# An ALiBi table built ahead of all attention, used by batch 1 in place of a bias matmul, and attention units that start earlier

## The chip, the cores and the metric

The kernel runs on one core of a Trainium2 chip. The metric is the time of one execution on the device in microseconds (us). The five engines of the core run side by side and wait for each other by semaphores: TensorE (PE, and PEld for its weight loads), VectorE (DVE), ScalarE (ACT), GpSimd (POOL) and SyncE (SP). Each takes its instructions in the order in which the program lists them.

## The reference

The inputs q, k and v are random fp32 of 8 batches, 8 heads, 576 positions and 64 columns; w_in is 512 x 2048 and w_out 2048 x 512.

```python
scores = (q @ k.T) / 8                        # for each batch and head
rel    = pos[:, None] - pos[None, :]
bias   = slopes[:, None, None] * -abs(rel)    # slopes[h] = 2 ** -(h + 1)
scores = where((rel >= 0) & (rel < 128), scores + bias, -1e9)
attn   = softmax(scores) @ v                  # sliding window of 128 keys
x      = attn.transpose(0, 2, 1, 3).reshape(4608, 512)
h      = x @ w_in                             # 4608 x 2048
out    = where(h > 0, h, exp(min(h, 0)) - 1) @ w_out
```

A query sees itself and the 127 keys before it. So a block of 128 keys meets 256 queries, and within these 256 columns the bias depends on the head alone.

## The kernel before

**Attention.** A batch has four units. Unit u holds, for all 8 heads, 128 keys by 256 queries (unit 3: 128 by 192 and the last 64 keys by 64). The scores of a unit go from TensorE into PSUM banks (spa, sp2, sp3), ScalarE writes their exponential to EX[u] in fp16 (L164, L169, L186), and TensorE multiplies by v with a column of ones (`values`, L207, result av). VectorE takes the reciprocal of the sum (L213) and normalises into xn (L214). `turn` transposes xn into the ring xT, by TensorE and a copy (L228, L229) for batch 0 and most of batch 1, by a transposing DMA issued on SP (L222) for the rest.

**Two ways of adding the bias.** Batches 0 and 1 go through `first_scores`. For each half of the heads it puts slope times RB, the masked distances, into the bank with four matmuls of 256 columns against SI, a scaled identity (L153), and adds q k to it (L159). Batches 2 to 7 go through `scores` and `expo` without a bias, and VectorE multiplies EX by a table of exponentials TAB afterwards (`weigh`, L191). TAB is made by ScalarE from RB, one activation for each head (`table`, L324), in slots 18 to 21.

**The MoE part.** 9 tiles of 512 tokens. `hidden` multiplies a step of x by w_in into one of the banks hp (L246; in early slots sp2 as well), ScalarE takes the exponential e (L251), POOL clamps it in place (L252), and VectorE makes g (L259, `elu`), which frees the bank. `output` multiplies four chunks of g by w_out (L268); after four such steps ScalarE copies the bank op to ob (L272) and SP sends it out.

**The order.** It is written out by hand. The program is a list of slots, one for each step of `hidden`: 16 slots to a tile of tokens, slot 16 t + j for step j of tile t. In a slot come first what `before` has put there (exponentials of attention), then `hidden`, then `elu` of the step one or two slots earlier, then what `at` has put there (scores, weighs, values, turns, loads), and at last `output`, whose step runs 17 slots behind `hidden`. The fourth of its four steps falls on every slot whose number is a multiple of 4.

A batch from 2 on has a start slot in START. Its unit u has scores at START[b] + 4 u, exponentials in the two slots behind, a weigh in each of the same two, values in the two after these, and the turn with the second values; a fifth block of values follows unit 3 two slots later. The K and Q transposes on VectorE (`turn_qk`, L131) come 8 to 1 slots before START[b], the loads of q, k and v, issued on POOL, 16 to 3 slots before it. Batch 1's units start at slots 10, 12, 14 and 16.

**The start.** POOL makes index tables with iota and issues the first loads; VectorE makes ident, RB and SI; TensorE runs 80 matmuls on ident (`warm`, L278), then transposes the first q and k (`turn_first`, L123), which VectorE and ScalarE copy to KT and QT (L127).

## Time and profile before

| | |
|---|---|
| median of 7 runs | 337.15 us (335.54 to 337.86) |
| the profiled execution | 336.41 us, span 334.6 us |
| granted TensorE clock in it | 1.0 |
| TensorE (PE) busy | 320.1 us, 96% |
| VectorE (DVE) busy | 214.2 us, 64% |
| ScalarE (ACT) busy | 184.5 us, 55% |
| POOL busy | 166.1 us, 50% |

The profile is one execution. A row of its timeline has the start in us, the duration in us, the engine, the line of the kernel, the operation, output and input with their shapes, how many instructions were merged, and in brackets the idle time of the engine before it with what ended that. The span is the time from the first instruction to the last; the execution's own time is 1.8 us longer.

### The profile page before, as it was taken

The page shows a single profiled execution, that of the slowest core. Times are in us where ns is not written, and L with a number is a line of the kernel's source. Part 1 is how long each engine was busy: PE and PEld are TensorE (multiplying, and loading weights), DVE is VectorE, ACT ScalarE, POOL GpSimd, SP SyncE. Part 2 cuts the span into 40 slices and gives each one's busy share as a digit, 9 for nine tenths or more (in the row PEclk, how much of TensorE's full clock was granted, in tenths as well). Part 3 has the DMA queues.
Part 4 walks back from the last instruction along what each step waited for, and adds up shares of the span by engine and source line. Part 5 has one row for each costly group of instructions (what it writes and reads, how often), then busy time and mean ns, then how long its engine had stood idle before and what let it go on. Part 6 is the DMA issues. An engine that isn't in the chain of part 4 may idle for free.

```text
span 334.6 us, 9249 instructions
## 1 busy us (share of the span) xinstructions
PE 320.1 (96%) x3884; PEld 226.2 (68%) x3884; DVE 214.2 (64%) x433; ACT 184.5 (55%) x325; POOL 166.1 (50%) x257
## 2 busy tenths in 40 slices
PE   8999989999997999899999999999999999999995
PEld 8777757767675667666667666666776666766542
DVE  5547546776697767886689667976699666644300
ACT  1666658756664566546565666656554666444311
POOL 8658756226664465535656465726665222333200
PEclk9999999999999999999999999999999999999999
DMA  8999999116999299946999298937999111110121
GB/s 108 197 197 166 194 191 91 12 41 90 118 113 69 56 132 108 103 73 89 123 90 101 58 124 107 109 83 107 122 98 89 55 50 49 47 41 31 50 78 63
DMA packets 93641, 31.99 MB, mean 96 GB/s; under 512 B 81824, under 2 KB 88992, under 8 KB 93600
## 3 DMA queue, kind: packets, MB, share of 16 engines
q0 software_dynamic: 73344, 18.36, 67.3%
q1 hardware_dynamic: 20256, 13.05, 15.1%
q8 instruction: 30, 0.49, 0.6%
q14 instruction: 11, 0.09, 0.1%
HBM read 36.70 MB, written 9.44 MB: 138 GB/s over the span
## 4 chain that ended last, share of the span: by engine, by line
PE 83%; DVE 5%; DMA 5%; ACT 3%; issue 2%; POOL 1%; DVEq 0%; ACTq 0%; POOLq 0%; SPq 0%
PE hp L246 32%; PE op L268 31%; DMA xT<-xn 5%; PE av L207 5%; PE spa L180 3%; PE spare L278 2%; PE hp L268 2%; PE spa L153 2%; DVE g L259 1%; DVE xn L214 1%; ACT e L251 1%; PE spa L159 1%; POOL e L252 1%; PE tp L123 1%; DVE KT L131 1%
## 5 line engine op out<-in xcount | busy, mean ns | idle before, releaser
L252 POOL TENSOR_SCALAR e<-e 128x512 f32<-128x512 f32 x144 | 89.5, 622 | 143.2 <-ACT e L251 142.5
L246 PEld LDWEIGHTS <-wi 128*128 128x128 f16 x1600 | 121.0, 98 | 43.1 <-issue 4.3
L246 PE MATMUL hp<-xT,wi 128*128 128x256 f16 (+3 forms) x1504 | 145.1, 245 | 3.1 <-DMA xT<-xn 2.9
L268 PE MATMUL op<-wo,g 128*128 128x512 f16 x544 | 138.6, 379 | 1.2 <-ACT ob L272 1.2
L251 ACT ACTIVATE e<-hp 128x512 f32<-128x512 f32 x139 | 83.3, 600 | 95.4 <-PE hp L246 91.9
L259 DVE SCALAR_TENSOR_TENSOR g<-e,hp 128x512 f16<-128x512 f32 x139 | 93.7, 674 | 65.6 <-POOL e L252 65.2
L268 PEld LDWEIGHTS <-g 128*128 128x128 f16 x576 | 50.6, 97 | 44.8 <-issue 5.4
L100 POOL DMA_DIRECT2D VP<-in_v_dram x40 | 35.1, 878 | 1.0 <-issue 0.7
L191 DVE TENSOR_TENSOR EX<-EX,TAB 128x1024 f16<-128x1024 f16 x48 | 32.8, 684 | 4.0 <-ACT EX L186 4.0
L214 DVE TENSOR_TENSOR xn<-av,rden 128x256 f16<-128x256 f32 (+1 forms) x79 | 33.4, 423 | 2.9 <-DVE rden L213 0.3
L207 PE MATMUL av<-VP,EX 128*128 128x65 f16 x572 | 30.0, 193 | 2.3 <-issue 1.1
L272 ACT COPY ob<-op 128x512 f32<-128x512 f32 x34 | 19.9, 585 | 20.9 <-PE op L268 20.9
L207 PEld LDWEIGHTS <-EX 128*128 128x128 f16 x576 | 26.6, 98 | 4.1 <-issue 1.7
L186 ACT ACTIVATE EX<-spa 128x512 f16<-128x512 f32 x48 | 26.1, 595 | 4.0 <-PE spa L180 3.4
L186 ACT ACTIVATE EX<-sp 128x512 f16<-128x512 f32 x48 | 26.1, 600 | 0.0
L213 DVE RECIPROCAL rden<-av 128x4 f32<-128x4 f32 (+1 forms) x79 | 13.9, 176 | 18.8 <-PE av L207 17.9
L131 DVE STREAM_TRANSPOSE KT<-st 128x576 f16<-128x576 f16 x24 | 19.6, 817 | 0.0
L131 DVE STREAM_TRANSPOSE QT<-st 128x576 f16<-128x576 f16 x24 | 19.6, 815 | 0.0
L164 ACT ACTIVATE EX<-spa 128x1024 f16<-128x1024 f32 (+1 forms) x16 | 13.9, 867 | 6.9 <-PE spa L159 6.8
L94 POOL DMA_DIRECT2D st<-in_q_dram x24 | 16.4, 682 | 1.0 <-DMA wo<-in_moe_w_out_dram 0.9
L94 POOL DMA_DIRECT2D st<-in_k_dram x24 | 16.4, 685 | 0.1
L180 PE MATMUL sp<-QT,KT 32*128 32x256 f16 (+2 forms) x240 | 14.7, 248 | 0.0
(62 smaller groups left out, 148.0 us busy)
## 6 DMA issues: line engine op xcount, KB each, us to landing
out_dram<-ob SPq DMA_DIRECT2D x36, 256.0 KB, 2.3
VP<-in_v_dram POOLq DMA_DIRECT2D x32, 128.0 KB, 4.6
st<-in_k_dram POOLq DMA_DIRECT2D x24, 144.0 KB, 3.6
st<-in_q_dram POOLq DMA_DIRECT2D x24, 144.0 KB, 3.7
wi<-in_moe_w_in_dram POOLq DMA_DIRECT2D x4, 512.0 KB, 11.3
wo<-in_moe_w_out_dram POOLq DMA_DIRECT2D x4, 512.0 KB, 10.3
s<-in_k_dram POOLq DMA_DIRECT2D x2, 384.0 KB, 9.7
s<-in_q_dram POOLq DMA_DIRECT2D x2, 384.0 KB, 10.2
```

What stands on the lines that cost most here:

```text
L94: nc.gpsimd.dma_start(st[b][32 * g:32 * g + 32, w, :, :, :, :].rearrange("p h n j d -> p (h n) (j d)"), (q, k)[w][b, 2 * g:2 * g + 2, :, : ...
L100: nc.gpsimd.dma_start(VP[b % 2][0:p, n, :, 0:D], v[b, :, 128 * n:128 * n + p, :].rearrange("h p d -> p h d"))
L131: V.transpose(o, st[b][:, w, h2, n0:n1, :, 32 * dh:32 * dh + 32])
L186: nc.scalar.activation(unit(b, u)[:, g, :, :], sp[g].rearrange("p (h c) -> p h c", h=2), AF.Exp, scale=0.125)
L191: V.tensor_tensor(out=e, in0=e, in1=TAB[:, int(u == 3), 2 * gp:2 * gp + 2, :, :], op=ALU.mult)
L207: nc.tensor.matmul(a[:, x, h2, :], ex_[u][:, c:c + 128], VP[b % 2][:, n, 2 * g + h2, 0:D + 1], start=j == 0, stop=j == len(parts) - 1)
L214: V.tensor_tensor(out=o, in0=a[0:m, :, :, 0:D], in1=r[0:m].unsqueeze(3).broadcast_to([m, 2, 2, D]), op=ALU.mult)
L246: nc.tensor.matmul(p[:, l * w + u0:l * w + u1], w_in_sb[:, c, fc * 128:(fc + 1) * 128], xT[:, c, x0:x0 + u1 - u0], start=(c == 0), stop=(c ...
L251: nc.scalar.activation(e[:, 0:n], p[:, 0:n], AF.Exp)
L252: nc.gpsimd.tensor_scalar(out=e[:, 0:n], in0=e[:, 0:n], scalar1=1.0, scalar2=0.0, op0=ALU.min, op1=ALU.max)
L259: V.scalar_tensor_tensor(out=gs[t][:, f0:f0 + nf, c0:c0 + w], in0=sh(es.pop((t, c0, f0))), scalar=1.0, in1=sh(hps.pop((t, c0, f0))), op0=A ...
L268: nc.tensor.matmul(o, gs[t][:, fc, ts * 128:(ts + 1) * 128], w_out_sb[:, fc, :], start=(fc == 0), stop=(fc == NFC - 1))
```

## The change

Three things change. First, RB is made from 256 columns in fp16 on VectorE, from the 128 columns of `col` that ident already needs; the other columns are copied, and three iota of POOL go. Second, the eight table activations stand ahead of the warm-up matmuls and all attention, and batch 1 and unit 3 of batch 0 take no bias matmuls: a new `first_weigh` multiplies their exponentials by TAB on VectorE, one slot after the scores of each half (both halves in slot 5 for batch 0). Third, START of batch 3 comes one slot sooner and that of batches 4 to 7 two slots sooner.

```diff
         def first_scores(b, u, half, d):
...
-            r0 = 256 * int(u == 3)
-            for x, hh in heads:
+            added = b == 0 and u < 3
+            for x, hh in heads if added else []:
                 c = 256 * (x % 2)
-                nc.tensor.matmul(sp[2 * d + hh][:, c:c + 256], SI[:, 4 * hh + x, :], RB[:, r0:r0 + 256],
+                nc.tensor.matmul(sp[2 * d + hh][:, c:c + 256], SI[:, 4 * hh + x, :], RB[:, 0:256],
                                  start=x % 2 == 0, stop=False, skip_group_check=True)
...
-                                     start=False, stop=True, skip_group_check=True)
+                                     start=not added, stop=True, skip_group_check=True)
...
+        def first_weigh(b, u, half):
+            e = unit(b, u)[:, half::2, :, :]
+            V.tensor_tensor(out=e, in0=e, in1=TAB[:, int(u == 3), half::2, :, :], op=ALU.mult)
...
-        rel = one([128, 512], I32, "rel")
...
-        for c, n in ((0, 256), (256, 192), (448, 64)):
-            nc.gpsimd.iota(rel[:, c:c + n], pattern=[[1, n]], base=0, channel_multiplier=-1)
...
-        ra = one([128, 512], F32, "ra")
-        V.tensor_scalar(out=ra, in0=rel, scalar1=0.0, scalar2=BIG, op0=ALU.is_lt, op1=ALU.mult)
-        V.tensor_tensor(out=ra, in0=ra, in1=rel, op=ALU.add)
-        rb = one([128, 512], F32, "rb")
-        V.tensor_scalar(out=rb, in0=ra, scalar1=127.0, scalar2=BIG, op0=ALU.is_gt, op1=ALU.mult)
-        V.scalar_tensor_tensor(out=RB, in0=ra, scalar=-1.0, in1=rb, op0=ALU.mult, op1=ALU.subtract)
+        rel = one([128, 256], F16, "rel")
+        off = one([128, 256], F16, "off")
+        V.tensor_scalar(out=rel[:, 0:128], in0=col, scalar1=rowf, scalar2=None, op0=ALU.subtract)
+        V.tensor_scalar(out=rel[:, 128:256], in0=rel[:, 0:128], scalar1=128.0, scalar2=None, op0=ALU.add)
+        V.tensor_scalar(out=off, in0=rel, scalar1=0.0, scalar2=-BIG, op0=ALU.is_lt, op1=ALU.mult)
+        V.tensor_tensor(out=off, in0=off, in1=rel, op=ALU.subtract)
+        V.tensor_scalar(out=rel, in0=rel, scalar1=127.0, scalar2=-BIG, op0=ALU.is_gt, op1=ALU.mult)
+        V.tensor_tensor(out=RB[:, 0:256], in0=off, in1=rel, op=ALU.add)
+        V.tensor_copy(RB[:, 256:448], RB[:, 0:192])
+        V.tensor_copy(RB[:, 448:512], RB[:, 0:64])
...
+        for h in range(H):
+            table(h)
         warm(80)
...
+        at(5, first_weigh, 0, 3, 0)
+        at(5, first_weigh, 0, 3, 1)
...
-        for h in range(H):
-            at(18 + h // 2, table, h)
...
                 at(a + half, first_scores, 1, u, half, 0)
                 before(a + half + 1, first_expo, 1, u, half, 0, 0, 256)
+                at(a + half + 1, first_weigh, 1, u, half)
                 at(a + half + 2, values, 1, u, half)
...
-        START = [None, None, 25, 41, 59, 77, 95, 113]
+        START = [None, None, 25, 40, 57, 75, 93, 111]
```

## The prediction

> **What bounds it now.** I read the page first, then the waits, then the chain that ended last, then the timeline around the code that changes.

> ```profile
> PE 320.1 (96%) x3884; PEld 226.2 (68%) x3884; DVE 214.2 (64%) x433; ACT 184.5 (55%) x325; POOL 166.1 (50%) x257
> ...
> PE hp L246 <- DMA xT<-xn: 2.9, 2, 1.9
> ...
> 100.08 6.11 DMA xT<-xn
> ```

> TensorE is the bound: 14.5 us of idle in 334.6, so only its own work, or what makes it wait, counts. The second line is from the waits: two stalls on a transposing transfer, the longest 1.9 us. I number slots by the runs of L246: slot 12 starts at 42.93 us, 19 at 60.75, 40 at 106.23, 56 at 140.48, and a late slot without attention takes 1.74. Slot 15, where batch 1 runs, is in the timeline (start, duration, engine, line):

> ```profile
> 51.39 1.07 PE L246 MATMUL hp<-xT,wi 128*128 128x128 f16 x16
> 51.56 1.02 ACT L164 ACTIVATE EX<-spa 128x1024 f16<-128x1024 f32 x1 [0.22 <-PE spa L159]
> ...
> 52.30 0.40 PE L207 MATMUL av<-VP,EX 128*128 128x65 f16 x8
> 52.50 0.60 ACT L251 ACTIVATE e<-hp 128x512 f32<-128x512 f32 x1
> ...
> 52.64 0.60 PE L153 MATMUL spa<-RB,SI 128*128 128x256 f16 x4
> 52.74 0.18 DVE L213 RECIPROCAL rden<-av 128x4 f32<-128x4 f32 x1 [0.77 <-PE av L207]
> 52.95 0.42 DVE L214 TENSOR_TENSOR xn<-av,rden 128x256 f16<-128x256 f32 x1
> 53.17 0.39 PE L159 MATMUL spa<-QT,KT 64*128 64x256 f16 x4
> ...
> 53.30 0.68 DVE L259 SCALAR_TENSOR_TENSOR g<-e,hp 128x512 f16<-128x512 f32 x1
> ```

> TensorE goes from one row to the next; VectorE has 1.3 us of work in a 2.1 us slot. L153 is what the change takes out.

> **Bias matmuls out, weighs in.** From L153 to L159 is 0.53 us, and 0.10 of it is the change of row groups, which stays: 0.43 us for four matmuls. Ten halves lose them (two of batch 0, eight of batch 1): 4.3 us at most. Each gets a multiply on VectorE of the form that L191 has (128x1024, mean 684 ns), between exponential and values. What waits behind it on VectorE: the next clamp-and-max (L259), reciprocal and normalisation, and behind those TensorE's next values. VectorE's rows overlap: L259 starts at 95.04 and the weigh after it at 95.65. So a slot costs VectorE 0.61 (L259) + 0.21 + 0.35 (L213 to L214 to the next) + 0.60 (weigh) = 1.8 us, against TensorE's 0.9 hidden + 0.25 values + 0.5 scores with its gaps + 0.1 for a turn in every second slot = 1.75. The two are level, so some is lost. By place:
> - Batch 0's last unit, slots 4 to 7: TensorE already waits there for xn (0.11 at 26.92), and two weighs stand ahead of the L259 that frees a bank for slot 7. Followed through the queues: -0.1, not -0.86.
> - Batch 1's first half, slot 10: -0.4. Its second: L159 waits 0.51 at 42.61 for the copy of KT, which hides the bias: 0. Third: -0.43. So -0.9 at slot 13.
> - The other five, slots 13 to 17: 5 x 0.43 = 2.15, less some 0.2 in each second slot where values wait for the weigh: -1.6. That is -2.5 at slot 18.

> **Given back in slot 19.** Two values share one bank there, and the next bank but one is ScalarE's:

> ```profile
> 61.86 0.40 PE L207 MATMUL av<-VP,EX 128*128 128x65 f16 x8
> ...
> 63.00 0.42 PE L207 MATMUL av<-VP,EX 128*128 128x65 f16 x8 [0.74 <-DVE xn L214]
> ...
> 65.70 1.14 ACT L324 ACTIVATE TAB<-RB 128x512 f16<-128x512 f16 x2
> ...
> 67.21 0.60 ACT L272 COPY ob<-op 128x512 f32<-128x512 f32 x1
> ...
> 67.86 1.02 PE L268 MATMUL op<-wo,g 128*128 128x512 f16 x4 [0.46 <-ACT ob L272]
> ```

> The last weigh of batch 1 comes ahead of a transpose of K and this normalisation on a VectorE with no idle since 60.30: the second values start 0.7 later, +0.7. The tables leave slots 18 to 21; with them goes the wait of 0.46 at 67.86 and a restart of about 0.1: -0.6. Front in all: -2.4.

> **The table at the start.** Eight activations, 1.14 a pair: 4.6 us. VectorE's chain to RB is now eight operations after 1.56 us. Their nearest rows are 0.15 (SI, 128 fp16 columns) and 0.85 (512 fp32 columns, L311); half of that for half the columns gives 0.15 to 0.45, so RB at 2.8 to 5.2 and the table at 7.4 to 9.8. I take 0.25 each, since the operands are short and fp16. ScalarE's first copy starts at 9.99, after the 80 warm-up matmuls end at 9.07, so it is hidden at both ends; without that cover it would cost 4.6. The three iota that go (0.74 on POOL) let loads start 0.7 sooner, but no load ends a wait of TensorE there: 0.

> **The moved units.** With a unit go its scores, exponentials, weighs, values, turn, loads and K/Q transposes. Batch 2 stays at slot 25.
> - Slots 48 and 56 wait 0.07 and 1.07 for the turn of a batch 3 unit, which comes one slot (1.74) sooner: -1.1.
> - Slot 40 waits 1.86 for batch 2's turn, not moved. But its 6.11 us lie beside two 128 KB loads of V for batch 3; one slot sooner, the second of them is the 64 KB one. Turns beside V loads took 2.3 to 5.5. The gain is 0 to 1.86, and below nothing if two other loads meet there (+0.3); I take -1.0.
> - Slot 43 now has both batch 2's last values and batch 3's first in one bank, as slot 19 has: 1.14 from start to start, less 0.25 of work: +0.9.
> - Batch 3's scores move from slots 41, 45, 49, 53 to 40, 44, 48, 52. Every fourth slot ends an output group, so ScalarE's copy ob (L272), which waits for that output, now stands ahead of the exponentials. Such a queue is in the trace at batch 4, for the second pair of heads:

> ```profile
> 167.24 0.58 ACT L272 COPY ob<-op 128x512 f32<-128x512 f32 x1 [0.31 <-PE op L268]
> 167.72 1.09 ACT L186 ACTIVATE EX<-sp 128x512 f16<-128x512 f32 x2
> ...
> 168.69 0.62 ACT L251 ACTIVATE e<-hp 128x512 f32<-128x512 f32 x1
> ```

> For the first pair: scores slot's first matmul at P, output ends P+2.8, ob P+2.9, exponentials P+3.4, e P+4.3, POOL's clamp P+5.0, L259 P+5.7 to P+6.4, and only then is the hp bank of the slot three later free, due at P+6.1. Wait 0.3, and 0.4 where a transpose of K or Q stands in VectorE's queue: +1.1 over slots 47, 51, 55 (43 has slack). Bounds: 0 (ScalarE catches up) and 0.75 each.
> - Batches 4 to 7 swap the positions 3, 1, 3, 1 (slot modulo 4) for 1, 3, 1, 3, and TensorE is full there: 0.

> **Sum.** -2.4 - 1.1 - 1.0 + 0.9 + 1.1 = -2.5. The profiled execution took 336.41 (span 334.6, 1.8 around it): it should become 333.9. The median of the runs, 337.15, is 0.74 above it; moved alike it is 334.6.

> [...] The clamp on POOL and a weigh met once in full:

> ```profile
> 112.61 1.26 POOL L252 TENSOR_SCALAR e<-e 128x512 f32<-128x512 f32 x1 [2.02 <-ACT e L251]
> 112.73 0.67 DVE L191 TENSOR_TENSOR EX<-EX,TAB 128x1024 f16<-128x1024 f16 x1
> ```

> The clamp took 1.26 and not 0.62, although it began first; all 48 weighs took 0.67 to 0.69. I charge the meeting to the clamp, which has a slot of slack. [...] Secondly, L259 runs until 95.73 and the weigh behind it starts at 95.65. [...]

> **Rivals.**
> - *VectorE keeps up*: nothing is held in slots 13 to 19, and all of batch 1's bias but the hidden half comes through: -3.0 - 0.1 - 0.6 instead of -2.4, with the rest as above: -3.8, 333.3; with no ob queue either, -4.9, 332.2. For it: VectorE at 60% from 50 to 60 us. Against: its loop is as long as TensorE's. 0.13.
> - *The weigh is held by the clamp* (slower). In slots 11 to 18 the exponential ends just when e is clamped (48.25 and 48.85 in slot 13), so they meet in every slot. 0.65 (1.26 less 0.61) on each of eight weighs, on the loop that values wait for: +5.2, in all +2.7, 339.8. It decides from 0.31 per weigh on (2.5/8). Against: no weigh of 48 was long, and batch 2 to 7 meet too. 0.13.
> - *Batch 3's position costs all that is won* (no change). Slots 47, 51 and 55 at 0.75 instead of 0.35 (+1.2), slot 43 also in the queue (+0.5), and slot 40 keeps its wait (+1.0): +2.7, so +0.2, 337.3. For it: the order on ScalarE is written in the code. 0.16.

> **Numbers.** Forecast 0.58, rivals 0.13, 0.13, 0.16. A measurement of this kernel tells about 0.3% (1.0 us) from no change. Forecast and first rival are nearly all faster; of the third, most is same: faster 0.72, same 0.15, slower 0.13. The range leaves out the first rival's far end and most of the second: 332.6 to 337.3.

> **To check.** L153 has 24 matmuls; slots 14 to 17 take 1.75 to 1.85 instead of 2.1 to 2.3; the two values of slot 19 lie 1.8 apart; no wait for ob at slot 21; no wait for xT at slot 56, but one for av at slot 43 and for hp at 47, 51, 55. Wrong if the rows of the added weigh are longer than 0.7 or the first copy of ScalarE starts after 10.0.

## The result, and the profile after

| | before | after |
|---|---|---|
| median of the runs, us | 336.75 (31 runs, 335.17 to 337.86) | 334.11 (12 runs, 332.36 to 335.15) |
| ratio, 95% interval | | 0.9919 [0.9902, 0.9935] |
| profiled execution, us (span) | 336.41 (334.6) | 332.67 (330.9) |

The change made the kernel faster by 0.8%; 334.6 was forecast. In the profiled execution the gain is 3.74 us where the sum said 2.5, in the medians 2.6. The two differences have causes of their own, found below.

The new function moves most lines behind it 4 further down: L246 is now L250, L207 L211, L214 L218, L259 L263, L272 L276, and L324 is L330; the new weigh is L175. First the page's line of engines, then three rows of the waits (us in total, times, longest).

```profile
PE 316.0 (96%) x3844; PEld 223.4 (68%) x3844; DVE 219.0 (66%) x447; ACT 182.8 (55%) x325; POOL 168.5 (51%) x254
```

```profile
PE av L211 <- DVE xn L218: 2.4, 2, 1.4
...
PE hp L250 <- DMA xT<-xn: 1.1, 2, 0.9
PE spa L159 <- DVE KT L127: 1.1, 1, 1.1
```

TensorE has 40 matmuls less (the ten halves of L153) and is busy 4.1 us less, VectorE 4.8 more. The waits for the transposing transfers fell from 2.9 to 1.1; the wait for a normalised unit rose from 0.7 to 2.4. In the chain that ended last the two turns before slots 32 and 40 stand like this (start, duration; before, the second took 6.11):

```profile
80.16 5.10 DMA xT<-xn
...
97.44 4.42 DMA xT<-xn
```

The end of slot 14 and slot 15 (from 48.26) in the timeline, with VectorE's chain and POOL's clamp:

```profile
46.81 1.15 POOL L256 TENSOR_SCALAR e<-e 128x512 f32<-128x512 f32 x1 [0.36 <-ACT e L255]
46.81 0.68 DVE L175 TENSOR_TENSOR EX<-EX,TAB 128x1024 f16<-128x1024 f16 x1
...
47.41 0.68 DVE L263 SCALAR_TENSOR_TENSOR g<-e,hp 128x512 f16<-128x512 f32 x1
...
48.04 0.18 DVE L217 RECIPROCAL rden<-av 128x4 f32<-128x4 f32 x1
...
48.26 0.42 DVE L218 TENSOR_TENSOR xn<-av,rden 128x256 f16<-128x256 f32 x1
48.26 1.07 PE L250 MATMUL hp<-xT,wi 128*128 128x128 f16 x16
...
48.60 0.81 DVE L175 TENSOR_TENSOR EX<-EX,TAB 128x1024 f16<-128x1024 f16 x1
48.87 1.01 POOL L256 TENSOR_SCALAR e<-e 128x512 f32<-128x512 f32 x1
49.34 0.68 DVE L263 SCALAR_TENSOR_TENSOR g<-e,sp 128x512 f16<-128x512 f32 x1
49.45 0.62 ACT L255 ACTIVATE e<-hp 128x512 f32<-128x512 f32 x1
49.47 0.29 PEld L211 LDWEIGHTS <-EX 128*128 128x128 f16 x8 [0.32 <-DVE EX L175]
```

From L263 to L263 VectorE needs 1.93 us and has no idle; the slot takes 1.88. Where a clamp and a weigh met, the clamp paid and sometimes both did: the clamps took 1.15 and 1.01 instead of 0.61, the weighs 0.68, which is as short as any, and 0.81. The last row is the values' wait for a weigh.

The start, and slot 19:

```profile
1.48 0.28 DVE L311 TENSOR_SCALAR rel<-col,rowf 128x128 f16<-128x128 int32 x1
...
3.54 0.30 DVE L318 COPY RB<-RB 128x64 f16<-128x64 f16 x1
...
3.88 4.26 ACT L330 ACTIVATE TAB<-RB 128x512 f16<-128x512 f16 x8 [1.86 <-DVE RB L318]
...
9.94 0.80 ACT L127 COPY QT<-hp 128x768 f16<-128x768 f16 x1 [1.79 <-PE hp L123]
```

```profile
57.44 0.68 DVE L175 TENSOR_TENSOR EX<-EX,TAB 128x1024 f16<-128x1024 f16 x1
58.04 0.82 DVE L131 STREAM_TRANSPOSE KT<-st 128x576 f16<-128x576 f16 x1
...
58.18 0.42 PE L211 MATMUL av<-VP,EX 128*128 128x65 f16 x8
58.76 0.65 DVE L263 SCALAR_TENSOR_TENSOR g<-e,hp 128x512 f16<-128x512 f32 x1
...
59.53 0.42 DVE L218 TENSOR_TENSOR xn<-av,rden 128x256 f16<-128x256 f32 x1
...
60.02 0.42 PE L211 MATMUL av<-VP,EX 128*128 128x65 f16 x8 [1.42 <-DVE xn L218]
```

The table is done at 8.14, 1.79 us before ScalarE's first copy. In slot 19 the first values wait for the weigh, and their normalisation stands behind a transpose of K and a clamp-and-max: the second values come 1.84 after the first.

### The profile page after: what moved, and what is told of

Its sections match the earlier page's. It is cut to its first block, busy times and chain, and to the rows that moved or that the text cites. A ratio compares the mean times of both kernels' runs of the same rounds, so it can differ in the third digit from the quotient of the medians.

```text
span 330.9 us, 9178 instructions
## 1 busy us (share of the span) xinstructions
PE 316.0 (96%) x3844; PEld 223.4 (68%) x3844; DVE 219.0 (66%) x447; ACT 182.8 (55%) x325; POOL 168.5 (51%) x254
## 3 DMA queue, kind: packets, MB, share of 16 engines
q1 hardware_dynamic: 20256, 13.05, 14.5%
## 4 chain that ended last, share of the span: by engine, by line
PE 75%; DVE 7%; DMA 7%; ACT 4%; issue 3%; POOL 3%; DVEq 0%; ACTq 0%; POOLq 0%
PE op L272 31%; PE hp L250 29%; PE av L211 4%; PE spa L184 3%; DMA wo<-in_moe_w_out_dram 3%; DMA xT<-xn 3%; DVE g L263 2%; POOL e L256 2%; PE spare L282 2%; PE hp L272 2%; DVE xn L218 1%; ACT EX L190 1%; ACT e L255 1%; DMA VP<-in_v_dram 1%; DVE KT L131 1%
## 5 line engine op out<-in xcount | busy, mean ns | idle before, releaser
L256 POOL TENSOR_SCALAR e<-e 128x512 f32<-128x512 f32 x144 | 92.8, 645 | 136.7 <-ACT e L255 135.8
L250 PEld LDWEIGHTS <-wi 128*128 128x128 f16 x1600 | 121.2, 98 | 42.3 <-issue 6.7
L250 PE MATMUL hp<-xT,wi 128*128 128x256 f16 (+3 forms) x1504 | 144.8, 245 | 1.7 <-DMA xT<-xn 1.1
L272 PE MATMUL op<-wo,g 128*128 128x512 f16 x544 | 138.6, 379 | 0.7 <-ACT ob L276 0.7
L263 DVE SCALAR_TENSOR_TENSOR g<-e,hp 128x512 f16<-128x512 f32 x139 | 93.6, 674 | 62.2 <-POOL e L256 60.8
L272 PEld LDWEIGHTS <-g 128*128 128x128 f16 x576 | 50.7, 97 | 44.3 <-issue 4.8
L218 DVE TENSOR_TENSOR xn<-av,rden 128x256 f16<-128x256 f32 (+1 forms) x79 | 33.4, 423 | 2.7
L276 ACT COPY ob<-op 128x512 f32<-128x512 f32 x34 | 19.9, 585 | 23.8 <-PE op L272 23.8
L211 PE MATMUL av<-VP,EX 128*128 128x65 f16 x572 | 29.9, 193 | 3.2 <-DVE xn L218 2.4
L211 PEld LDWEIGHTS <-EX 128*128 128x128 f16 x576 | 26.2, 98 | 5.5 <-DVE xn L218 2.6
L164 ACT ACTIVATE EX<-spa 128x1024 f16<-128x1024 f32 (+1 forms) x16 | 14.0, 876 | 3.1 <-PE spa L159 3.0
```

The costliest lines, as they stand in the source:

```text
L211: nc.tensor.matmul(a[:, x, h2, :], ex_[u][:, c:c + 128], VP[b % 2][:, n, 2 * g + h2, 0:D + 1], start=j == 0, stop=j == len(parts) - 1)
L218: V.tensor_tensor(out=o, in0=a[0:m, :, :, 0:D], in1=r[0:m].unsqueeze(3).broadcast_to([m, 2, 2, D]), op=ALU.mult)
L250: nc.tensor.matmul(p[:, l * w + u0:l * w + u1], w_in_sb[:, c, fc * 128:(fc + 1) * 128], xT[:, c, x0:x0 + u1 - u0], start=(c == 0), stop=(c ...
L256: nc.gpsimd.tensor_scalar(out=e[:, 0:n], in0=e[:, 0:n], scalar1=1.0, scalar2=0.0, op0=ALU.min, op1=ALU.max)
L263: V.scalar_tensor_tensor(out=gs[t][:, f0:f0 + nf, c0:c0 + w], in0=sh(es.pop((t, c0, f0))), scalar=1.0, in1=sh(hps.pop((t, c0, f0))), op0=A ...
L272: nc.tensor.matmul(o, gs[t][:, fc, ts * 128:(ts + 1) * 128], w_out_sb[:, fc, :], start=(fc == 0), stop=(fc == NFC - 1))
```

## Where the time went, slot by slot

Differences of slot lengths between the two profiled executions, beside the terms of the sum. A slot is counted here from its first weight load, so a wait ahead of its first matmul is in it where that load had already begun.

| place | forecast | measured |
|---|---|---|
| batch 0, unit 3 (start of slot 7) | -0.1 | -0.10 |
| slot 10 | -0.4 | -0.44 |
| slot 11 | 0 | -0.08 (the wait for K's copy grew from 0.51 to 1.06) |
| slot 12 | -0.43 | -1.71 (a stall of 1.10 is gone) |
| slots 13 to 17 | -1.6 | -1.62 |
| slot 19 | +0.7 | +1.02 |
| slot 21 | -0.6 | -0.62 |
| front (start of slot 22) | -2.4 | -3.61 |
| wait before slot 32 | 0 | +0.96 |
| wait before slot 40 | -1.0 | -1.69 |
| slot 43 | +0.9 | +0.98 of wait |
| slots 47, 51, 55 | +1.1 | +1.04 (0.31, 0.37, 0.36) |
| waits before 48 and 56 | -1.1 | -1.14 |
| to the end | -2.5 | -3.74 |

The rows leave -0.28 over, which no single place shows: it is spread over work that now sits in other slots and batches 4 to 7. In slots 47, 51 and 55 the 0.24 of values that moved there from other slots is taken out first: slot 47 grew from 1.74 to 2.29, less 0.24 leaves 0.31.

## The experiments

The theory was the sum's: the front gains by the bias matmuls' going, and the move of the units gives and takes about the same. Rivals: the weigh is held by the clamp; the move alone, or a stall that the sum had left out, makes the time. Ratios are against the kernel before, timed beside each run.

**Front and units apart.** First the changed kernel with the positions of before.

```diff
-        START = [None, None, 25, 40, 57, 75, 93, 111]
+        START = [None, None, 25, 41, 59, 77, 95, 113]
```

> The table at the start and the weighs in place of batch 1's bias matmuls, with the start slots of before. The prediction's sum gives the front -2.4 us, and slot 40 and 56 keep the waits of before (1.9 and 1.1): about -2.4 against before. If the stall of 1.1 us in slot 12 of the profile of before is chance and not part of the change, the timed difference stays near -2.4 while a profile may show up to -3.6 at slot 22. Rival (VectorE keeps up): -3.7. Rival (the weigh is held by the clamp): above 0.

Measured: 334.45 us, 0.9952 [0.9931, 0.9974]. Then the kernel before with the new positions (the same line the other way):

> The kernel before with only the new start slots. Prediction's parts: waits of slots 48 and 56 gone (-1.1), slot 40's wait shorter (-1.0, in the profile of the changed kernel -1.7), two values in one bank at slot 43 (+0.9, in that profile +1.3), ob ahead of the exponentials at slots 47, 51, 55 (+1.1, in that profile +1.8): -0.1 by the prediction, +0.2 by the profile of the changed kernel. Rival (batch 3's position costs all that is won): +2.5 or more.

Measured: 336.27 us, 1.0013 [0.9992, 1.0033]. So the front carries the gain, but less of it than the sum's 2.4: alone it brings 1.6, the move alone costs 0.4, which the interval does not tell from nothing, and both together bring 2.7 (0.0081 of 336): more than their sum. The waits say why. TensorE's row for the transposing transfers in the run with the front alone, and one more wait, before slot 88, that the profile names otherwise although it ends 0.09 us after such a transfer has landed (203.20):

```profile
PE hp L250 <- DMA xT<-xn: 3.0, 3, 1.5
```

```profile
203.29 1.03 PE L250 MATMUL hp<-xT,wi 128*128 128x256 f16 x8 [1.05 <-DVE KT L131]
```

With the front alone TensorE waits 4.1 us for transfers, where the kernel before waits 2.9; with the units moved as well it waits 1.1. From slot 22 to the end the front alone so gives back 1.04, and the changed kernel gives back nothing (-0.13).

**Batch 3 one slot later** in the changed kernel (40 becomes 41 in START), and then also its V loads one slot sooner:

> The changed kernel with batch 3 at slot 41 as before; batches 4 to 7 keep their new slots. If the ob queue and the shared bank of values are what slots 43, 47, 51, 55 cost (3.0 us in the profile of the changed kernel), all four waits go; slot 56 gets back about 1.1 and slot 40 up to 1.7, since V loads come a slot later: -0.3 against the changed kernel, and no wait for hp at slots 47 to 55. If the waits came from something else (the DMA or VectorE's load in general), they stay and the time rises by 1 to 2.8 us.

Measured: 333.0 us, 0.9915 [0.9888, 0.9943]. Slots 43, 47 and 51 are back at 1.98, 1.74 and 1.76, as forecast, and the waits for transfers are back as well (first row below): no difference from the changed kernel that the intervals show.

```diff
-                at(a - 12 + n if b == 2 else a - 7 + n, load_v, b, n)
+                at(a - 12 + n if b == 2 else a - 7 - (b == 3) + n, load_v, b, n)
```

> As the run with batch 3 at slot 41, but its five V loads are issued one slot sooner, in the slots that they have in the changed kernel. If slot 40's wait is set by which V load lies beside batch 2's turn, the wait stays at 0 to 0.4 us as in the changed kernel: 1.3 us faster than the run before it, -1.6 against the changed kernel. If the V loads do not set it, the same as the run before it.

Measured: 332.74 us, 0.9917 [0.9886, 0.9949]. A miss: the waits moved to other slots (0.25 before slot 40, 1.20 before 48, 1.87 before 56) and their sum stayed. The rows of the two runs:

```profile
PE hp L250 <- DMA xT<-xn: 3.1, 3, 1.6
```

```profile
PE hp L250 <- DMA xT<-xn: 3.3, 3, 1.9
```

So the term "-1.0 at slot 40, by another V load beside the turn" has the wrong cause. The wait at slot 40 is 0.13 to 0.34 in all seven traces of kernels without batch 1's bias matmuls whose turn there is a transfer, also with the front alone, where units and V loads stand as before (0.34); it is 1.26 to 1.86 in all five traces with them, also where the units have moved (1.34). The fall belongs to the front. What in the front brings it is below, under "Why a transfer is late".

**The start alone, and the weighs alone.** The kernel before with the new RB and the table ahead of attention; then the same with the ten weighs added while the bias matmuls stay, so that the bias counts twice.

```diff
+        at(5, first_weigh, 0, 3, 0)
+        at(5, first_weigh, 0, 3, 1)
...
+                at(a + half + 1, first_weigh, 1, u, half)
```

> The changed kernel's start alone: RB from 256 fp16 columns and the table ahead of attention, while batch 1 and batch 0's unit 3 keep their bias matmuls, no weigh is added and the units stand where they stood before. By the prediction's sum only the table's leaving slots 18 to 21 counts: -0.6 us against the kernel before (slot 21 loses its wait for ob), nothing at the start, slots 13 to 17 stay at 2.1 to 2.3 and slot 19 at 3.15 less what the table held. Rival (start not hidden): ScalarE's first copy later than 10.0 us and every slot later by as much. Of the stall of 1.1 us that TensorE shows in slot 12 of the kernel before with nothing that it waits for: if it belongs to the longer code of the bias matmuls it stays here (slot 12 about 4.1); if it was made by what stood on POOL's queue (three iota) it goes and the time falls by 1.7.

Measured: 336.11 us, 1.0002 [0.998, 1.0024]. The profile has -0.61 at slot 22, all of it slot 21 (2.38 to 1.76), and no delay at the start; in the time it can't be seen. The stall stays (1.22 at 46.18), so neither the table nor POOL's three iota made it.

> The same, and the ten weighs of batch 1 and of batch 0's unit 3 are added although the bias matmuls stay, so the bias counts twice in these units. What the weighs cost by themselves, against the run without them: by the prediction +0.7 in slot 19 and some 0.2 in each second slot of 13 to 17, and some 0.7 at slots 4 to 7 of batch 0: +1.5 to +2.3 us. If the weigh is held by POOL's clamp (second rival): 0.65 on each of eight weighs, +5 us. If VectorE keeps up (first rival): under +0.8, with slot 19 as before.

Measured: 336.31 us, 1.0015 [0.9991, 1.0039]. Slots 13 to 17 are as long as before (2.10, 2.23, 2.10, 2.27, 2.71); slot 19 takes 3.71 instead of 3.15:

```profile
L175 DVE TENSOR_TENSOR EX<-EX,TAB x10: 681/688/1043, 28.0 to 60.3; 128x1024 f16<-128x1024 f16 x10
```

```profile
62.98 0.42 PE L211 MATMUL av<-VP,EX 128*128 128x65 f16 x8 [1.30 <-DVE xn L218]
```

The first row (min/median/max in ns) ends the rival of the held weigh: of the ten one took 1.04, three 0.81 to 0.82, and six 0.68 to 0.69, which is 0.08 more on the mean than the shortest, where the rival needed 0.31. The weighs cost 0.56 in slot 19 and nothing in slots 13 to 17, which still have their bias matmuls; +5 was the rival's price. They cost less than the +1.5 to +2.3 expected, too: in the profile the stall of slot 12 is 0.50 shorter than in the run without them (0.72), and at slot 22 the two are level.

**Two waits of the front taken out.** Batch 1's last values one slot later, and in slot 11 the scores ahead of the turn of K:

```diff
-        at(11, turn_first, 1, 1, 1, 0, sp[3], V.tensor_copy)
...
                 at(a + half, first_scores, 1, u, half, 0)
+                if a + half == 11:
+                    at(11, turn_first, 1, 1, 1, 0, sp[3], V.tensor_copy)
...
-        at(19, values, 1, 4, 0)
-        at(20, values, 1, 4, 1)
-        at(21, turn, 1, 4)
+        at(20, values, 1, 4, 0)
+        at(21, values, 1, 4, 1)
+        at(22, turn, 1, 4)
```

> The changed kernel with two moves in its front: batch 1's last two values one slot later (slots 20 and 21, their turn in 22), so that slot 19 no longer has two values in one bank; and in slot 11 the scores ahead of the transposes of K, whose copy they waited for (1.06 us at 41.93). If the wait of 1.42 us in slot 19 comes from the shared bank, as the prediction has it, slot 19 falls from 4.17 to about 2.7; if it comes from VectorE being behind on the weighs, slots 20 and 21 take it over. If the wait in slot 11 hides the bias, as the prediction has it, then slot 11 falls from 3.31 to about 2.3 here, where there is no bias to hide. Both right: -2.0 us against the changed kernel (about 332.1 where that takes 334.1), less what the transposing transfers before slots 32 and 40 then make TensorE wait.

Measured: 330.81 us, 0.9857 [0.9829, 0.9884]. Slot 19 fell from 4.17 to 2.12, with 0.41 of it given back in slots 20 and 21 (the values' own work): the shared bank was the cause. Slot 11 fell from 3.31 to 2.53, yet its gain was lost two slots later:

```profile
43.63 0.79 PE L250 MATMUL sp<-xT,wi 128*128 128x128 f16 x11
45.99 0.71 PE L250 MATMUL sp<-xT,wi 128*128 128x128 f16 x5 [1.57 <-issue]
```

So the profile is no shorter than that of the changed kernel (331.1 against 330.9; it has a stretch at half clock, see below). The medians differ very likely because four of its five runs had a clock of 0.998 or more, which one of the changed kernel's twelve had.

**The turns on TensorE.** The same with batch 3 at slot 41, and the turns of units 0 and 2 of batches 2 and 3 as matmuls with a copy on ScalarE:

```diff
-                at(a + 4, turn, b, u)
+                if b in (2, 3) and u in (0, 2):
+                    at(a + 5, turn, b, u, nc.scalar.copy, "av")
+                else:
+                    at(a + 4, turn, b, u)
```

> The same, with batch 3 starting at slot 41 and the four turns that slots 32, 40, 48 and 56 wait for (batches 2 and 3, units 0 and 2) done by TensorE and a copy on ScalarE one slot later, instead of by a transposing DMA. Theory: the moved units gain or lose through these waits and through the position of the scores in the group of four slots; so here the waits for xT at slots 32, 40, 48 and 56 (0.96, 0.13, 1.58, 0.55 in the run with batch 3 at 41) are gone, slots 43, 47, 51 and 55 wait for nothing, and TensorE pays 4 x 0.3: -2.0 against the run before this one's place (batch 3 at 41), with the front's -2.0 in all -4 against the kernel with batch 3 at 41 and against the changed kernel: about 330. Rival: the transfers' waits only hide others (banks of hp, VectorE's queue), and the time falls by under 1 us from the front's mend.

Measured: 328.55 us, 0.9773 [0.9749, 0.9797]. No wait for xT is left, slots 43, 47, 51 and 55 take 1.98, 1.74, 1.76 and 1.76, and each turn costs TensorE 0.22. So the waits for transfers are what the moved units trade in, and no other wait stood behind them.

**The output's copy ahead of the exponentials.** The changed kernel with three copies ob (those of slots 44, 48 and 52) on VectorE:

```diff
-                nc.scalar.copy(ob, o)
+                (V.tensor_copy if (t, ts) in ((1, 2), (1, 3), (2, 0)) else nc.scalar.copy)(ob, o)
```

> The changed kernel with three of the output copies ob, those of slots 44, 48 and 52, on VectorE instead of ScalarE, where they stand ahead of batch 3's exponentials. If that copy in ScalarE's queue is what makes slots 47, 51 and 55 longer, as the prediction has it, they fall from 2.29, 2.37 and 2.36 to 1.74 to 1.8 and their waits for hp (0.15 to 0.21) go: some -1.5 us at slot 56, less what its transposing transfer then makes it wait. Rival: VectorE's own queue (the weigh and the transposes of K and Q ahead of L263) is what holds the bank; then the copy on VectorE makes these waits longer.

Measured: 331.77 us in a single run, which settles nothing in the time; its profile does. Slots 47, 51 and 55 took 1.98, 2.00 and 2.00, that is 1.74 to 1.76 and the 0.24 of values, and their waits are gone. From slot 43 to 56 that is 0.88, where 1.5 was expected: the expectation had counted the values' 0.24 as a wait. The chain in the changed kernel, slots 49 to 51, is ob, exponentials, e, clamp, L263, and TensorE behind it:

```profile
122.94 0.58 ACT L276 COPY ob<-op 128x512 f32<-128x512 f32 x1 [1.21 <-PE op L272]
...
123.42 1.09 ACT L190 ACTIVATE EX<-spa 128x512 f16<-128x512 f32 x2
...
124.39 0.62 ACT L255 ACTIVATE e<-hp 128x512 f32<-128x512 f32 x1
...
125.09 0.62 POOL L256 TENSOR_SCALAR e<-e 128x512 f32<-128x512 f32 x1 [2.03 <-ACT e L255]
...
125.88 0.65 DVE L263 SCALAR_TENSOR_TENSOR g<-e,hp 128x512 f16<-128x512 f32 x1
...
126.59 0.49 PE L250 MATMUL hp<-xT,wi 128*128 128x192 f16 x4 [0.21 <-DVE g L263]
```

**The stall that the sum left out.** In the kernel before, and in the changed one:

```profile
46.16 0.20 PE L207 MATMUL av<-VP,EX 128*128 128x65 f16 x1 [1.10 <-issue]
```

```profile
45.64 0.45 PE L250 MATMUL sp<-xT,wi 128*128 128x128 f16 x5 [0.18 <-issue]
```

TensorE waits for nothing that the profile names. But in the nine traces so far that have such a stall it stands ahead of the same place in TensorE's work, its 864th weight load and matmul (some 1729 rows from the start), and that place is passed between 45.4 and 46.2 us, however early TensorE gets there. The DMA queue 8 carries instructions in packets of 16 KB (30 packets, 0.49 MB on the page), and the profile does not say whose. In the kernel before, TensorE starts 166 to 318 rows from one packet to the next, while the time between them goes from 4.3 to 18.5 us; so they are taken for its instructions. There these packets begin at 24.5, 30.9, 37.9 and 43.9 us, 6.0 to 7.0 us apart, while the loads fill the DMA engines (busy 90% or more in every slice from 24 to 50 us). And the stalled row follows the last of them: in each of the nine traces it starts 1.27 to 1.49 us after the packet that began at 42.8 to 43.9 has ended.

The next run issues three of the four loads of w_out some slots later, in the kernel before:

```diff
-        for n in range(4):
-            at(5 + n, load_wo, n)
+        for n, s in enumerate((5, 12, 13, 14)):
+            at(s, load_wo, n)
```

> The kernel before with one edit: three of the four loads of w_out (512 KB each) are issued in slots 12, 13 and 14 instead of 6, 7 and 8. It tests what the 1.10 us stall of TensorE at 46.16 is, which the prediction's sum left out. Theory: TensorE's instruction stream comes in 16 KB packets on queue 8, one every 6.2 us while the loads fill the DMA engines (24 to 50 us), and in all nine profiles the stall stands ahead of the same row of TensorE, the 1729th, which none of them passes before 45.4 us: a fetch slowed by the loads. Then here the packets from 30 us on come closer together than 6.2 us, the 1729th row starts without a stall at about 45.1, and slot 12 takes 3.0 instead of 4.13: -1.1 us in the front (-0.5 to -1 in the time, as the wait at slot 40 takes some of it). Rival: the fetch has its own pace, whatever the DMA engines carry; then the stall stays at 1.1 and the time is the same.

Measured: 334.48 us, 0.9951 [0.9935, 0.9968]. The packets come at 37.1, 42.1 and 46.7, and the stall, which was expected to go, is halved; the row starts 1.31 after the packet's end. Of the 1.2 us by which the profile is shorter the stall makes 0.53; 0.41 stands ahead of slot 0, where nothing was changed.

```profile
45.15 0.20 PE L207 MATMUL av<-VP,EX 128*128 128x65 f16 x1 [0.57 <-issue]
```

> The same edit in the kernel with the front mended and the four turns on TensorE, which shows a stall of 1.00 us at 45.38. Theory (the loads slow the fetch): the stall goes, -1.0 us: 327.5 where that kernel takes 328.5. Rival (own pace): no change. Both: if a late load of w_out holds an output of slots 18 to 20, a wait for wo shows there, and the gain is lost.

Measured: 327.5 us, 0.9747 [0.9727, 0.9767], the fastest of all. The packets come at 30.8, 36.2, 41.1 and 45.6, and the stall is gone. Against 0.9773 the intervals overlap, so the last 0.3% is not shown; the stall's going is. Nor do the profiles show a gain (326.0 against 326.1): 0.58 comes back in slot 14, where values now wait for a weigh, and 0.30 more stands ahead of slot 0.

**Why a transfer is late.** No run was made for this; the kept traces tell it. TensorE's instruction packets also lie beside the transposing transfers. In the five traces with the bias matmuls of batch 1 a packet begins 1.9 to 2.4 us into the transfer that slot 40 waits for, and the transfer takes 5.50 to 6.11 us. In the seven without them none lies beside it, and it takes 4.38 to 4.58. Here are the rates of all transfers together (GB/s in 40 slices from that transfer's issue to its landing), in the kernel before with the packet's row, then with the front alone:

```profile
GB/s 308 268 201 228 145 110 81 122 145 147 151 115 169 259 238 252 49 12 20 10 10 1 6 10 8 10 12 76 146 157 157 158 138 154 160 84 0 0 0 0
...
q8 instruction: 1, 0.02, 1.0%
```

```profile
GB/s 286 268 303 196 232 150 159 46 143 123 142 154 160 152 162 142 126 208 245 207 174 118 86 97 111 117 116 109 133 111 138 91 16 10 7 0 0 0 91 58
```

Before, the traffic all but stops for some 1.5 us, from the time at which the packet comes; with the front alone it runs on. Over all 14 traces, 180 of 426 such transfers have a packet beside them, and all 46 that took over 4.9 us are among these. So a packet beside a transfer is very likely what makes it long. As no run moved the packets alone, it is not shown, and many transfers with a packet were not long. With batch 1's bias matmuls gone the later packets lie elsewhere against the work: in the kernel before one begins at 102.5 us, 2.4 into the transfer at 100.08; in the changed kernel that packet begins at 103.1, 1.2 after the transfer at 97.44 has landed.

**Why the medians gained less than the profile.** The changed kernel's profile has a mean granted clock of 1.0, but 11 of its 12 runs had 0.988 to 0.995. The last run tests whether the stall brings that:

> The changed kernel with the loads of w_out in slots 5, 12, 13 and 14 and nothing else changed. What is open is why the changed kernel's profiled execution (332.67 us at a granted clock of 1.0) lies 1.4 below the median of its runs: 11 of its 12 runs had a mean clock of 0.988 to 0.995, and the profiles that show 0.995 have one stretch of 3.3 us at half clock between 43 and 50 us, where TensorE idles for K's copy and for its instructions. Theory: the stretches come from that idle time; with the loads out of the way the instructions come sooner, the runs have clock 1.0 (as all seven and four runs with late loads had), the stall of 0.18 goes, and the median falls from 334.1 to about 332.4, 0.989 of the kernel before, in a range of under 1.5 us. Rival: the stretches belong to the changed front itself (the weighs, the wait of 1.06 in slot 11, which stays here); then the clock stays at 0.99 in most runs and the median at 334.

Measured: 333.96 us, 0.9935 [0.9912, 0.9958]. The theory fell for this kernel: no stall is left in the profile, and 8 of 12 runs still have 0.988 to 0.994. The four at 1.0 took 331.88 to 332.68. The profiled run has 0.989, and shows where (busy time of PE, PEld, DVE, ACT and POOL with their instructions, then the granted clock, the DMA share and GB/s):

```profile
40.00:41.00 1.00, 0.63 (x39) 0.53 (x33) 0.34 (x1) 0.37 (x1) 1.00 (x2) 1.00 1.77 180
41.00:42.00 1.00, 0.32 (x4) 0.12 (x5) 1.00 (x2) 0.00 (x0) 0.98 (x3) 1.00 1.15 115
42.00:43.00 1.00, 1.00 (x14) 1.00 (x13) 0.82 (x2) 0.83 (x1) 0.92 (x2) 0.63 1.65 162
43.00:44.00 1.00, 1.00 (x21) 0.80 (x20) 0.00 (x0) 0.47 (x2) 0.00 (x0) 0.50 1.40 125
...
48.00:49.00 1.00, 1.00 (x10) 0.59 (x11) 0.95 (x3) 0.77 (x2) 0.52 (x1) 0.50 1.22 201
49.00:50.00 1.00, 1.00 (x22) 1.00 (x21) 1.00 (x2) 0.80 (x2) 1.00 (x3) 0.95 1.27 174
```

TensorE runs at half clock from 42.3 to 49.1 us, right after the wait for K's copy in slot 11 (1.05 us at 41.68). Slot 13 takes 2.58 there instead of 1.80. In four other profiles such a stretch lasts 3.4 us (0.995). Two of them (the front alone, the copies on VectorE) have the same wait and begin 2.0 us after it. The other two (the move alone, the mended front) have a shorter wait there; they begin at 46.7 and 45.9, just behind or in the stalls for instructions of 1.27 and 1.57 us, which end at 45.8 and 46.0. So the stall may bring a stretch as well. By the clocks of the runs: of 48 runs of the five kernels that have the wait of 1.06 us (the changed one, the front alone, batch 3 at 41, the same with early V loads, late w_out), 31 had 0.995 or less and 23 had 0.990 or less (a sixth, with the copies on VectorE, had one run, at 0.995). Of 75 runs of the kernel before (wait 0.51, stall 1.10), 31 and none; of the 7 with late loads of w_out (stall 0.57), none. Of 13 runs of the three kernels without that wait (0.28 there), one and none. The kernel with the mended front differs from the changed one ahead of 50 us only in slot 11's order. So the longer wait is the likely cause of clocks of 0.990 and less; that the kernels ran on different chips in part leaves it short of shown, and a run with slot 11's order alone was not made.

## Why the prediction was right, and where it was not

- **Front: -2.4, measured -3.61.** The other terms (slots 7, 10, 13 to 17, 21) came out within 0.05. The 0.10 between matmuls on 128 rows and scores on 64 stands in the changed kernel's rows: 0.35 from values to scores (51.37 to 51.72), 0.25 from values to a matmul on 128 rows (60.02 to 60.27). The "restart of about 0.1" is 0.16: slot 21 lost 0.62, of which 0.46 was the wait. The step that failed is slot 12, "Third: -0.43": the stall of 1.10 us in that slot of the trace before was never mentioned. Twenty matmuls and their weight loads are gone ahead of the stalled place, so it lies further on in the work: TensorE reached it at 45.46 instead of 45.06, the packet had ended at 44.15 instead of 44.88, and a stall of 0.18 was left.
- **Slot 19: +0.7, measured +1.02.** The second values' wait was sized right (0.74 to 1.42, +0.68); the first values' own wait for the weigh, 0.27 at their weight loads, had not been counted.
- **Slot 11: 0 in the sum, and right there.** But the bias gone from under the wait made an idle of 1.06 out of 0.51, and with it most runs lost clock. How much that is, the kernel with late loads of w_out shows: 334.13 to 335.06 at 0.988 to 0.990, 331.88 to 332.68 at 1.0, some 2.4 us between the medians. This is very likely why the medians show 2.6 and not 3.7, and why 334.6 came so near 334.11: a stall not foreseen and a loss of clock not foreseen, of opposite signs. The nearness is luck.
- **Table at the start: hidden, right.** RB at 3.84 and the table at 8.14, inside the bounds of 2.8 to 5.2 and 7.4 to 9.8; the eight operations took 0.23 to 0.41.
- **Moved units: -0.1 in the sum; -0.13 from slot 22 to the end.** Slots 43, 47, 51, 55, 48 and 56 were right in mechanism and size. The row for slot 40 was -1.69, not -1.0, and it is the front's: the V loads that the term went by did not set that wait. A wait of 0.91 before slot 32 came unforeseen: its transfer was issued 3.61 earlier, as all else there, but took 5.10 us instead of 4.13. In the other traces of kernels without the bias matmuls whose turn there is a transfer it took 3.98 to 5.17; what sets it stays open. So the moved units' sum came out by misses of opposite signs, which is luck again.
- **Rivals.** "VectorE keeps up" holds in slots 13 to 18 nearly, not in 19. "The weigh is held": its mechanism exists (0.81 beside a clamp, where 0.68 is the shortest), but the eight weighs of batch 1 took 0.77 on the mean: 0.09 more, where the rival decided from 0.31 on. The prediction's sign of being wrong, rows of the added weigh longer than 0.7, is met by five of the eight (0.75 to 0.89), so that limit was set too close. "Batch 3's position costs all": its terms were there (+0.98 and +1.04); slots 48 and 56 repaid 1.14 of them, and slot 40's fall, from the front, the rest.
- **Clamp, weigh and VectorE's rows.** A clamp and a weigh that started together at 46.81 took 1.15 and 0.68, and the clamp begun 0.27 after a weigh took 1.01, the weigh 0.81. Beside 0.61, the median clamp, and 0.68, the shortest weigh, that is 0.54 and 0.40 more for the clamp, nothing and 0.13 more for the weigh: in neither case did one wait for the whole of the other. VectorE's rows overlap in that slot: but for the normalisation, which needs the reciprocal, each operation starts 0.05 to 0.08 before the end of the one ahead (47.41 + 0.68 against 48.04).

## What to carry to other kernels

Look at the idle time that the profile puts down to nothing as closely as at the named waits: a stall that stands ahead of one fixed row in every trace was very likely the instruction stream here, and fewer instructions ahead of it (1.10 us to 0.18), or fewer loads beside it (1.10 to 0.57), made it shorter; with both it was gone. When work was removed from under a wait that hid it, the wait grew by as much (0.51 to 1.06, where 0.53 of bias was gone); here that very likely cost clock as well, so mend the wait in the same change. The time of a transfer beside others is no constant: the same turn took 4.4 to 6.1 us. Before a change of the order is priced by such a wait, look in several traces at what lies beside the transfer, the instruction packets too.

## What the runs showed of the hardware that was not expected

The half-clock stretches (granted clock 0.50) lasted 3.4 or 6.8 us; half of that is what they can cost at most, an estimate: 1.7 us for 0.005 of the mean clock. What starts one is not shown. In the changed kernel with late loads of w_out TensorE had been busy in 0.95 us of the two before 42, where the clock then fell (0.63 from 42 to 43), and in all of the two before that. In the profile of the changed kernel itself it was busy in 0.94 us of the same two, and in all of the two before, and the clock stayed at 1.0.
